# GEGLU feed-forward kernel: another order of the seven products in the gate/up loop, and one copy instead of two for the last output block

## Chip, cores, metric

The kernel runs on one core of one Trainium2 chip. The metric is device time in microseconds (us), as the median of several runs. The span of a profile, from the first to the last instruction, is some 1.8 us shorter than the time of the same run (277.88 against 276.1 us before).

Names of the engines in the profile: PE is TensorE, which does the matmuls; PEld its weight loads; DVE is VectorE; ACT is ScalarE; POOL is GpSimd; SP is SyncE. The granted clock is the share of the full TensorE clock that the chip allowed; it is 1.0 or just below in every run here. A PSUM bank is a piece of the memory into which matmuls add. fp32r is the kernel's four-byte type for matmuls (`float32r`); the profile prints it as f32.

A verdict needs 2%. The change is worth less than that, so most of this document works in nanoseconds inside the profile, where the parts of the kernel that the change does not touch agree to a few nanoseconds from kernel to kernel.

## The reference, cut to what matters

```python
B, S, D, F = 32, 32, 1024, 3584          # all bf16
def reference(x, w_gate, w_up, w_down):
    return (_gelu(x @ w_gate) * (x @ w_up)) @ w_down
```

With tokens flattened, `x` is 1024 x 1024, gate and up are 1024 x 3584, down is 3584 x 1024.

## The kernel before

The kernel replaces eight block products by seven (a Strassen-Winograd scheme), once for gate and up together and once for down. The first four feature tiles are computed plainly. The other 24 go through the gate/up loop, and that is where the change is. A feature tile has seven products of four matmuls each, 128x128 weights against 128x512 moving data. Five take sums in fp32r, two take the bf16 inputs as they are. Condensed to the products, with comments of mine:

```python
# in one feature tile ft (cut); names P1..P7 are used below
prod(psa, a11, b11, True)      # P1  bf16   -> copied by ACT (sn1), then P6 adds onto the bank
prod(psc, s1, t1, True)        # P5  fp32r  -> copied by ACT (sn5), then P3 adds onto the bank
last_product(open_ft)          # P4  fp32r  (a22, t4) of the tile before, onto its psa
prod(psa, s2, t2, False)       # P6  fp32r  -> copied by ACT (sn2)
prod(psc, s4, b22r, False)     # P3  fp32r  -> DVE: c12 = sn2 + psc; ACT: gelu
prod(psb, a12, b21, True)      # P2  bf16   -> DVE: c11 = sn1 + psb; ACT: gelu
prod(psa, s3, t3, False)       # P7  fp32r  -> DVE: c22 = sn5 + psa, times the gelu
```

`psa` is one of three PSUM banks, `psb` and `psc` each one of two. P1, P6, P7 and P4 of a tile all add onto one `psa`, each after the copy or the read of what stood there. `snap` is a copy by ACT, `added` a sum by DVE. POOL meanwhile makes the sums s1 to s4 of the next two tiles.

The last output block, after the last product of the down projection:

```python
for m in range(MT):                                  # four blocks of 128 rows
    o = opool.tile([P, NB], bf16, name="o_sb", tag="o_sb")
    r0 = NB + m * P
    for i, (cast, eng) in enumerate(((nc.scalar.copy, nc.sync), (nc.vector.tensor_copy, nc.scalar))):
        c = slice(i * NB // 2, (i + 1) * NB // 2)
        cast(o[:, c], banka[m][:, c])
        eng.dma_start(out=of[r0 : r0 + P, c], in_=o[:, c])
```

Of the kernel before, what the change touches and what calls it, by code (L numbers as in the profile page):

```python
# [13 lines left out]
def kernel(  # L14
# [20 lines left out]
    nc = tc.nc  # L35
    P = nc.NUM_PARTITIONS
# [7 lines left out]
    of = out.flatten_outer_dims()  # L44
    N, D = xf.shape
    F = w_gate.shape[1]
    NB = 512
    assert N == 2 * NB and D == 2 * NB and F % (4 * P) == 0
    DT, FT = D // P, F // P
    KD = DT // 2  # L50
    FC = 2
    F0 = 4
# [46 lines left out]
    def g_of(ft):  # L99
        k = ft % HF  # L100
        return by_batch(g_lo if ft < HF else g_hi)(k)

    def acc(tag):
        return ps1.tile([P, NB], fp32, name=f"ps{tag}", tag=tag, bufs={"A": 3, "B": 2, "C": 2, "G": 1}[tag])


    b11 = xpool.tile([P, KD, NB], bf16, name="b11")
    b21 = xpool.tile([P, KD, NB], bf16, name="b21")
    b12 = ring.tile([P, KD, NB], bf16, name="b12", tag="ring")
    b22 = ring.tile([P, KD, NB], bf16, name="b22", tag="ring")  # L110
    t1, t2, t3, t4, b22r = (xpool.tile([P, KD, NB], f32r, name=n) for n in ("t1", "t2", "t3", "t4", "b22r"))
# [21 lines left out]
    def load_w_chunk(ci):  # L133
        alloc_w(ci)
        for which in (0, 1):
            load_w(nc.sync, ci, which, 0, DT)

    def quads(ci, fl=None):
        cols = slice(None) if fl is None else slice(fl * P, (fl + 1) * P)
        wg, wu = w_tiles[ci]  # L140
        return wg[:, :KD, cols], wg[:, KD:, cols], wu[:, :KD, cols], wu[:, KD:, cols]

    def chunk_of(ft):
        ci, fl = divmod(ft - F0, FC)
        return ci + 1, fl
# [3 lines left out]
    def sums(ci, eng):  # L149

        a11, a12, a21, a22 = quads(ci)
        s1, s2, s4, s3 = (
            spool.tile([P, KD, FC * P], f32r, name=n, tag=n) for n in ("s1", "s2", "s4", "s3")
        )
        s_tiles[ci] = (s1, s2, s3, s4)
        yield eng.tensor_tensor(s1, a21, a22, ADD)  # L156
        yield eng.tensor_tensor(s2, s1, a11, SUB)  # L157
        yield eng.tensor_tensor(s4, a12, s2, SUB)  # L158
        yield eng.tensor_tensor(s3, a11, a21, SUB)  # L159
# [3 lines left out]
    def a22r_of(ft):  # L163
        t = spool.tile([P, KD, P], f32r, name="a22r", tag="a22r", bufs=3)
        nc.scalar.copy(t, quads(*chunk_of(ft))[3])  # L165
        a22rs[ft] = t
# [10 lines left out]
    with tc.manual_schedule():  # L177
        for eng, p0, p1 in ((nc.sync, 0, HALF), (nc.scalar, HALF, NB_P)):
            eng.dma_start(  # L179
                out=x_nat[:, p0:p1, :],  # L180
                in_=xf[p0 * P : p1 * P, : KQ * P].rearrange("(b p) d -> p b d", p=P),
# [84 lines left out]
        def prod(ps, lhs, rhs, start):  # L266
            for k in range(KD):
                nc.tensor.matmul(  # L268
                    ps,
                    lhsT=lhs[:, k, :],  # L270
                    rhs=rhs[:, k, :],
                    start=(start and k == 0),
                    stop=(k == KD - 1),
                    skip_group_check=True,
                )

        def snap(ps, tag, bufs):
            t = ework.tile([P, NB], fp32, name=tag, tag=tag, bufs=bufs)
            nc.scalar.copy(t, ps)  # L279
            return t  # L280

        def added(s, ps):
            t = ework.tile([P, NB], fp32, name="c", tag="c", bufs=3)
            tt(t, s, ps, ADD)  # L284
            return t

        def last_product(st):
            ft, psa, h0 = st
            prod(psa, a22rs.pop(ft), t4, False)
            tt(g_of(ft)[:, :NB], h0, psa, MUL)  # L290

        open_ft = None
        for ft in range(F0, FT):
            ci, fl = chunk_of(ft)
            fs = slice(fl * P, (fl + 1) * P)
            if fl == 0:
                nxt = sums(ci + 1, nc.gpsimd) if ci + 1 < NCH else iter(())
                if ci + 2 < NCH:
                    load_w_chunk(ci + 2)
            a11, a12, a21, a22 = quads(ci, fl)  # L300
            s1, s2, s3, s4 = (s[:, :, fs] for s in s_tiles[ci])
            psa, psc, psb = acc("A"), acc("C"), acc("B")
            prod(psa, a11, b11, True)
            sn1 = snap(psa, "sn1", 2)
            prod(psc, s1, t1, True)
            sn5 = snap(psc, "sn5", 2)
            if ft + FC < FT:
                a22r_of(ft + FC)
            if open_ft:
                last_product(open_ft)  # L310
            next(nxt, None)
            prod(psa, s2, t2, False)
            sn2 = snap(psa, "sn2", 1)
            prod(psc, s4, b22r, False)
            c12 = added(sn2, psc)
            h1 = acc("G")
            nc.scalar.activation(h1, c12, ACT.Gelu_apprx_tanh)  # L317
            prod(psb, a12, b21, True)
            c11 = added(sn1, psb)
            h0 = ework.tile([P, NB], bf16, name="h", tag="h")  # L320
            nc.scalar.activation(h0, c11, ACT.Gelu_apprx_tanh)
            next(nxt, None)
            prod(psa, s3, t3, False)
            c22 = added(sn5, psa)
            tt(g_of(ft)[:, NB:], c22, h1, MUL)
            open_ft = (ft, psa, h0)
# [84 lines left out]
        banka = [acc(t) for t in "AAAG"]  # L411
# [70 lines left out]
        for m in range(MT):  # L482
            o = opool.tile([P, NB], bf16, name="o_sb", tag="o_sb")
            r0 = NB + m * P
            for i, (cast, eng) in enumerate(((nc.scalar.copy, nc.sync), (nc.vector.tensor_copy, nc.scalar))):
                c = slice(i * NB // 2, (i + 1) * NB // 2)
                cast(o[:, c], banka[m][:, c])  # L487
                eng.dma_start(out=of[r0 : r0 + P, c], in_=o[:, c])
# [1 line left out]
_INS = ['x', 'w_gate', 'w_up', 'w_down']  # L490
_OUTS = [((32, 32, 1024), 'bfloat16')]
# [25 lines left out]
```

## Time and profile before

| | before |
|---|---|
| device time | 278.07 us, 3 runs, 277.82 to 278.48 |
| span of the profile | 276.1 us, granted clock 1.0 |
| start to start of two feature tiles | 6.327 us in the steady loop |
| last matmul's start to the span's end | 4.00 us |

The page of the kernel before: busy time of each engine (us, share of the span, instructions), and below it the first line of the chain of waits that ended last.

```profile
PE 271.4 (98%) x1207; PEld 182.5 (66%) x1207; DVE 173.3 (63%) x186; ACT 117.1 (42%) x181; POOL 94.8 (34%) x51
...
PE 96%; DMA 2%; ACTq 0%; DVE 0%; ACT 0%; issue 0%
```

TensorE (PE) bounds the kernel: the others have time to spare, and the chain hardly leaves PE. A busy PE is not a PE at its best pace, though. Ends of matmuls are estimated: so says the Trainium skill, "Perfetto Trace Analysis", section "Tensor Engine Instruction (MATMUL, LD_WEIGHTS)". This trace fits it. Matmuls that start 227 ns apart are each shown as 389 ns long. The section covers weight loads too, so the lengths of weight loads below are lengths in the profile and not measured times. So busy time and mean duration say nothing of the pace, and one has to look at starts.

The timeline of PE, before: start (us), length, line, operation, tiles, shape, count. One row is one product.

```profile
103.25 1.07 PE L268 MATMUL psA<-t,a22r 128*128 128x512 f32 x4
104.15 1.07 PE L268 MATMUL psA<-t,s 128*128 128x512 f32 x4
105.06 1.07 PE L268 MATMUL psC<-b22r,s 128*128 128x512 f32 x4
105.97 1.04 PE L268 MATMUL psB<-b,wg 128*128 128x512 bf16 x4
106.66 1.28 PE L268 MATMUL psA<-t,s 128*128 128x512 f32 x4
107.78 1.04 PE L268 MATMUL psA<-b,wg 128*128 128x512 bf16 x4
108.46 1.27 PE L268 MATMUL psC<-t,s 128*128 128x512 f32 x4
109.57 0.62 PE L268 MATMUL psA<-t,a22r 128*128 128x512 f32 x2
```

These are P4, P6, P3, P2, P7, P1, P5 and P4 again (the end of the window cuts the last row); bf16 comes in two groups of four, which I call islands. The first P7 matmul after an island appears to start only 0.69 us after the island's first, and then to last longer. That is an early-recorded start, not a fast product: island and following product together take 1.81 us (105.97 to 107.78).

Weight loads on the page of before, in bf16 and in fp32r: count, busy us, mean ns of one, idle before.

```profile
L268 PEld LDWEIGHTS <-wg 128*128 128x128 bf16 x192 | 15.0, 98 | 24.0 <-issue 12.5
...
L268 PEld LDWEIGHTS psA<-t,a22r 128*128 128x128 f32 x96 | 18.0, 188 | 3.9
```

The waits of weight loads in the loop, before: us in total, times, longest.

```profile
PEld L268 <- issue: 12.5, 47, 0.3
...
PEld psA L268 <- ACT sn L279: 0.2, 1, 0.2
PEld psC L268 <- ACT sn L279: 0.2, 1, 0.2
```

A bf16 load takes 98 ns, an fp32r load 188 ns. The Trainium skill, "TensorE: Matmul & The Clock Gate", section "Weight-path perf modes — Fast Weight Load (FWL) and DoubleRow", has the fast load on for 128 weights that are not FP32, with about a factor of two measured. The page does not say whether fp32r counts as FP32; the ratio in this trace, 188 to 98 or 1.9, fits if it does. The 47 "issue" waits mark the 47 places in the loop where fp32r gives way to bf16. Only two waits in the whole loop are for another engine, both at its start.

The timeline at the end, before: ACT copies its half, DVE waits for ACT, then the second store is issued.

```profile
272.53 0.37 ACT L487 CAST o_sb<-psG 128x256 bf16<-128x256 f32 x1 [1.21 <-PE psG L346]
272.93 0.33 SPq L488 DMA_DIRECT2D out_dram<-o_sb  x1
272.93 0.42 DVE L487 CAST o_sb<-psG 128x256 bf16<-128x256 f32 x1 [1.16 <-ACT o_sb L487]
273.39 0.34 ACTq L488 DMA_DIRECT2D out_dram<-o_sb  x1
```

### The profile page before, as it was taken

The page shows a single profiled execution, that of the slowest core. Times are in us where ns is not written, and L with a number is a line of the kernel's source. Part 1 is how long each engine was busy: PE and PEld are TensorE (multiplying, and loading weights), DVE is VectorE, ACT ScalarE, POOL GpSimd, SP SyncE. Part 2 cuts the span into 40 slices and gives each one's busy share as a digit, 9 for nine tenths or more (in the row PEclk, how much of TensorE's full clock was granted, in tenths as well). Part 3 has the DMA queues.
Part 4 walks back from the last instruction along what each step waited for, and adds up shares of the span by engine and source line. Part 5 has one row for each costly group of instructions (what it writes and reads, how often), then busy time and mean ns, then how long its engine had stood idle before and what let it go on. Part 6 is the DMA issues. An engine that isn't in the chain of part 4 may idle for free.

```text
span 276.1 us, 3300 instructions
## 1 busy us (share of the span) xinstructions
PE 271.4 (98%) x1207; PEld 182.5 (66%) x1207; DVE 173.3 (63%) x186; ACT 117.1 (42%) x181; POOL 94.8 (34%) x51
## 2 busy tenths in 40 slices
PE   8999999999999999999999999999999999999994
PEld 3444467666666777776666667754447888888883
DVE  0059975455555554554555555546999999999501
ACT  4034465555655555556556555430200022972001
POOL 1000069996765849494947650000000000000000
PEclk9999999999999999999999999999999999999999
DMA  7999023150505143250508500004992344686202
GB/s 156 318 249 263 3 76 104 51 154 0 154 1 151 34 118 96 58 143 10 154 0 251 168 2 1 0 0 135 348 318 76 111 155 167 234 271 206 77 6 70
DMA packets 52768, 33.77 MB, mean 122 GB/s; under 512 B 8720, under 2 KB 52752, under 8 KB 52752
## 3 DMA queue, kind: packets, MB, share of 16 engines
q1 hardware_dynamic: 49760, 31.20, 39.3%
q10 hardware_dynamic: 2992, 2.36, 2.8%
q8 instruction: 9, 0.15, 0.2%
q14 instruction: 7, 0.06, 0.1%
HBM read 29.62 MB, written 2.10 MB: 115 GB/s over the span
## 4 chain that ended last, share of the span: by engine, by line
PE 96%; DMA 2%; ACTq 0%; DVE 0%; ACT 0%; issue 0%
PE psA L268 32%; PE psC L268 16%; PE psA L346 14%; PE psB L268 8%; PE psB L346 7%; PE psC L346 7%; PE psG L346 5%; PE psA L221 4%; PE psB L221 3%; PE psC L221 2%; DMA wu<-in_w_up_dram 2%; PE psG L221 1%; ACTq L131 0%; ACTq L179 0%; DVE o_sb L487 0%; ACT o_sb L487 0%
## 5 line engine op out<-in xcount | busy, mean ns | idle before, releaser
L268 PE MATMUL psA<-t,s 128*128 128x512 f32 x192 | 56.4, 416 | 0.0
L268 PEld LDWEIGHTS psA<-t,s 128*128 128x128 f32 x192 | 36.1, 188 | 9.6 <-ACT sn L279 0.2
L279 ACT COPY sn<-psA 128x512 f32<-128x512 f32 x48 | 28.2, 588 | 21.5 <-PE psA L268 21.5
L156 POOL TENSOR_TENSOR s<-wu 128x1024 fp32r<-128x1024 bf16 x11 | 23.6, 2146 | 29.8 <-PE psC L268 29.8
L284 DVE TENSOR_TENSOR c<-sn,psC 128x512 f32<-128x512 f32 x24 | 16.5, 688 | 25.9 <-PE psC L268 25.9
L268 PEld LDWEIGHTS <-wg 128*128 128x128 bf16 x192 | 15.0, 98 | 24.0 <-issue 12.5
L268 PE MATMUL psC<-t,s 128*128 128x512 f32 x96 | 30.5, 439 | 0.0
L268 PE MATMUL psA<-t,a22r 128*128 128x512 f32 x96 | 25.9, 391 | 0.0
L268 PE MATMUL psC<-b22r,s 128*128 128x512 f32 x96 | 25.7, 389 | 0.0
L317 ACT ACTIVATE psG<-c 128x512 f32<-128x512 f32 x24 | 14.5, 602 | 25.6 <-DVE c L284 25.6
L268 PE MATMUL psB<-b,wg 128*128 128x512 bf16 x96 | 24.9, 382 | 0.0
L268 PE MATMUL psA<-b,wg 128*128 128x512 bf16 x96 | 24.9, 381 | 0.0
L158 POOL TENSOR_TENSOR s<-wg,s 128x1024 fp32r<-128x1024 bf16 x11 | 23.7, 2156 | 0.9
L157 POOL TENSOR_TENSOR s<-s,wg 128x1024 fp32r<-128x1024 f32 x11 | 23.6, 2146 | 0.9
L159 POOL TENSOR_TENSOR s<-wg,wu 128x1024 fp32r<-128x1024 bf16 x11 | 23.6, 2145 | 0.0
L290 DVE TENSOR_TENSOR hi<-h,psA 128x512 bf16<-128x512 bf16 x14 | 9.6, 688 | 19.5 <-PE psA L268 19.5
L268 PEld LDWEIGHTS psC<-t,s 128*128 128x128 f32 x96 | 18.1, 189 | 5.5
L268 PEld LDWEIGHTS psA<-t,a22r 128*128 128x128 f32 x96 | 18.0, 188 | 3.9
L268 PEld LDWEIGHTS psC<-b22r,s 128*128 128x128 f32 x96 | 17.9, 188 | 3.8 <-ACT sn L279 0.2
L284 DVE TENSOR_TENSOR c<-sn,psA 128x512 f32<-128x512 f32 x24 | 16.5, 688 | 5.8 <-PE psA L268 5.8
L284 DVE TENSOR_TENSOR c<-sn,psB 128x512 f32<-128x512 f32 x24 | 16.5, 687 | 2.8
L165 ACT CAST a22r<-wu 128x512 fp32r<-128x512 bf16 x24 | 14.9, 622 | 6.8 <-PE psA L268 6.8
(100 smaller groups left out, 419.8 us busy)
## 6 DMA issues: line engine op xcount, KB each, us to landing
wg<-in_w_gate_dram SPq DMA_DIRECT2D x12, 512.0 KB, 3.9
wu<-in_w_up_dram SPq DMA_DIRECT2D x12, 512.0 KB, 5.1
wdb<-in_w_down_dram SPq DMA_DIRECT2D x12, 512.0 KB, 4.7
wdb<-in_w_down_dram SPq DMA_DIRECT2D x12, 384.0 KB, 4.3
v<-in_w_down_dram SPq DMA_DIRECT2D x4, 512.0 KB, 6.1
v<-in_w_down_dram SPq DMA_DIRECT2D x4, 384.0 KB, 7.1
out_dram<-o_sb ACTq DMA_DIRECT2D x12, 128.0 KB, 1.7
wg<-in_w_gate_dram SPq DMA_DIRECT2D x3, 256.0 KB, 3.8
```

The costliest lines, as they stand in the source:

```text
L156: yield eng.tensor_tensor(s1, a21, a22, ADD)
L157: yield eng.tensor_tensor(s2, s1, a11, SUB)
L158: yield eng.tensor_tensor(s4, a12, s2, SUB)
L159: yield eng.tensor_tensor(s3, a11, a21, SUB)
L165: nc.scalar.copy(t, quads(*chunk_of(ft))[3])
L221: nc.tensor.matmul(ps, lhsT=w_tiles[0][which][:, dt, fl * P : (fl + 1) * P], rhs=x_rows(dt, nb), start=(dt == 0), stop=(dt == DT - 1),)
L268: nc.tensor.matmul(ps, lhsT=lhs[:, k, :], rhs=rhs[:, k, :], start=(start and k == 0), stop=(k == KD - 1), skip_group_check=True,)
L279: nc.scalar.copy(t, ps)
L284: tt(t, s, ps, ADD)
L290: tt(g_of(ft)[:, :NB], h0, psa, MUL)
L317: nc.scalar.activation(h1, c12, ACT.Gelu_apprx_tanh)
L346: nc.tensor.matmul(banks[m], lhsT=lhs(k)[:, m * P : (m + 1) * P], rhs=rhs(k), start=(start and k == 0), stop=(k == HF - 1), skip_group_che ...
```

## The change

Its intent: P2 of a tile and P1 of the next stand side by side, so that TensorE changes between bf16 and fp32r twice a tile instead of four times. P6 goes ahead of P4 as well. The last block is copied whole, by DVE and ACT in turn, and stored by one queue.

```diff
+        def first_product(ft):
+            psa = acc("A")
+            prod(psa, quads(*chunk_of(ft))[0], b11, True)
+            return psa, snap(psa, "sn1", 2)
+
         open_ft = None
+        ahead = first_product(F0)
         for ft in range(F0, FT):
   ... (cut)
-            psa, psc, psb = acc("A"), acc("C"), acc("B")
-            prod(psa, a11, b11, True)
-            sn1 = snap(psa, "sn1", 2)
+            (psa, sn1), psc, psb = ahead, acc("C"), acc("B")
             prod(psc, s1, t1, True)
             sn5 = snap(psc, "sn5", 2)
+            next(nxt, None)
+            prod(psa, s2, t2, False)
+            sn2 = snap(psa, "sn2", 1)
             if ft + FC < FT:
                 a22r_of(ft + FC)
             if open_ft:
                 last_product(open_ft)
-            next(nxt, None)
-            prod(psa, s2, t2, False)
-            sn2 = snap(psa, "sn2", 1)
             prod(psc, s4, b22r, False)
   ... (cut)
             next(nxt, None)
+
+            if ft + 1 < FT:
+                ahead = first_product(ft + 1)
             prod(psa, s3, t3, False)
   ... (cut)
-            for i, (cast, eng) in enumerate(((nc.scalar.copy, nc.sync), (nc.vector.tensor_copy, nc.scalar))):
-                c = slice(i * NB // 2, (i + 1) * NB // 2)
-                cast(o[:, c], banka[m][:, c])
-                eng.dma_start(out=of[r0 : r0 + P, c], in_=o[:, c])
+            (nc.vector.tensor_copy if m % 2 == 0 else nc.scalar.copy)(o, banka[m])
+            nc.scalar.dma_start(out=of[r0 : r0 + P, :NB], in_=o)
```

More of the change, by code (lines that the diff above doesn't have):

```diff
@@ L299 @@
                     load_w_chunk(ci + 2)
-            a11, a12, a21, a22 = quads(ci, fl)
             s1, s2, s3, s4 = (s[:, :, fs] for s in s_tiles[ci])
-            psa, psc, psb = acc("A"), acc("C"), acc("B")
-            prod(psa, a11, b11, True)
-            sn1 = snap(psa, "sn1", 2)
+            (psa, sn1), psc, psb = ahead, acc("C"), acc("B")
             prod(psc, s1, t1, True)
             sn5 = snap(psc, "sn5", 2)
+            next(nxt, None)
+            prod(psa, s2, t2, False)
+            sn2 = snap(psa, "sn2", 1)
             if ft + FC < FT:
@@ L317 @@
             nc.scalar.activation(h1, c12, ACT.Gelu_apprx_tanh)
-            prod(psb, a12, b21, True)
+            prod(psb, quads(ci, fl)[1], b21, True)
             c11 = added(sn1, psb)
```

## The prediction

> **What bounds the kernel now.** TensorE. The page gives PE 98% of the span at granted clock 1.0; the chain of waits is 96% PE; DVE, ACT and POOL are busy 63%, 42% and 34%. In the gate/up loop (32.7 to 183.7 us, 24 feature tiles of 28 matmuls) PE never waits for another engine but for two 0.2 us waits of weight loads at its start. Moving products can help only through what matmuls themselves cost, and hurt only by a new wait.
>
> **What the matmuls cost.** Ends of matmuls are modelled (the Trainium skill, "Perfetto Trace Analysis", section "Tensor Engine Instruction"), so I use distances between starts in the timeline. A feature tile takes 6.327 us in every steady iteration. Within fp32r products a matmul follows the last by 227 ns (weight load 188 ns); within bf16 products by 216 ns (weight load 98 ns). The shorter bf16 load agrees with "TensorE: Matmul & The Clock Gate", section "Weight-path perf modes": fast weight load is on for 128 weights that are not FP32. Pure pace would be 20 x 227 + 8 x 216 = 6.26 us. The other 65 ns are four changes of type: into bf16 the first two distances are 230 and 226; out of it 454 for two, then 233, 236 (or 231), 228. A bf16 island costs some 23 to 38 ns over its pace. There are 47 islands (the weight loads' "issue" idle: 47 times, 12.5 us; not PE time).
>
> **What the change does.** No matmul or copy of the loop is added or removed. P2 of a tile and P1 of the next form one island of eight, so 23 islands go. Built from the distances of before, an iteration becomes 6.29 to 6.30 us: 27 to 38 ns less, times 23 = 0.6 to 0.9 us, all on the critical path.
>
> **New waits?** I find none. Between P1 and P6 (which must wait for the copy of P1's bank) still lie two products, 1.8 us. ACT does that copy after the second gelu: ending 2.2 us after P2's end, with P6 starting 2.7 us after it: 0.5 us of slack, the tightest of all. P5 to P3, and P7 to P4, keep two products between; P6 to P7 gets four. Three A banks suffice. POOL's sums (four of 2.15 us in 12.65 us) end in time.
>
> **The tail.** Before, the two half copies of the last block run in series, since both write one tile: ACT 372 ns, then DVE 424 ns, then issue, 1.62 us to landing. After: one ACT copy of 512 columns (588 ns for that shape elsewhere), then a 128 KB store, 1.70 to 1.74 us to landing. 0.21 saved less 0.1: about 0.1 us gained.
>
> **Prediction.** 278.07 - 0.75 - 0.1 = 277.2 us, 8 in 10 within 276.6 to 277.8. Faster by over 2%: 1%; within 2%: 97%; slower by over 2%: 2%.
>
> **What would show the steps right or wrong.** Iteration distance 6.29 to 6.30 us; "issue" idle of weight loads 24 times, not 47; 216 ns across the seam P2 to P1; no wait of PE or its loads for ACT or DVE in the loop; last ACT copy about 0.59 us, the span's end about 0.1 us closer to the last matmul.
>
> **What would make it wrong.** A PE wait for the copy of P1 (ACT order) repeated 23 times: each 0.1 us would cost 2.3 us. Then: P7 after an island dearer than P5, which puts the gain at the lower end. Or a tail in which the ACT queue holds up the last copy behind an issue (0.34 us each).

## The result, and the profile after

| | before | after |
|---|---|---|
| device time, median | 278.04 us, 6 runs, 277.16 to 278.48 | 276.83 us, 6 runs, 276.33 to 277.01 |
| span of the profile | 276.1 us | 275.2 us |
| start to start of two feature tiles | 6.327 us | 6.300 us |
| last matmul's start to the span's end | 4.00 us | 3.61 us |

The ratio is 0.9958, 95% interval 0.9941 to 0.9975: the mean time of the fast runs after over that of the fast runs before in the same rounds, so not quite the ratio of the two medians. The time is inside the predicted range, and the sign is clear of noise.

The page after, the same lines:

```profile
PE 270.1 (98%) x1190; PEld 184.3 (67%) x1207; DVE 173.1 (63%) x184; ACT 114.4 (42%) x179; POOL 94.9 (34%) x51
...
PE 98%; issue 0%; ACT 0%
```

PE lacks 17 of its 1207 matmul records here; the weight loads are complete, so I take iteration times from the loads of P4. The timeline of PE, after:

```profile
103.92 1.07 PE L268 MATMUL psA<-t,a22r 128*128 128x512 f32 x4
104.82 1.07 PE L268 MATMUL psC<-b22r,s 128*128 128x512 f32 x4
105.73 1.04 PE L268 MATMUL psB<-b,wg 128*128 128x512 bf16 x4
106.61 1.03 PE L268 MATMUL psA<-b,wg 128*128 128x512 bf16 x4
107.28 1.27 PE L268 MATMUL psA<-t,s 128*128 128x512 f32 x4
108.39 1.08 PE L268 MATMUL psC<-t,s 128*128 128x512 f32 x4
109.31 1.07 PE L268 MATMUL psA<-t,s 128*128 128x512 f32 x4
110.22 0.62 PE L268 MATMUL psA<-t,a22r 128*128 128x512 f32 x2
```

P4, P3, then P2 and P1 as one island, P7, P5, P6. The next P4 comes 6.30 us after the first. The waits of weight loads in the loop, after:

```profile
PEld L268 <- issue: 6.3, 24, 0.3
...
PEld psA L268 <- ACT sn L279: 0.2, 1, 0.2
PEld psC L268 <- ACT sn L279: 0.2, 1, 0.2
```

ACT's timeline around the copy of P1's bank, after:

```profile
101.23 0.63 ACT L324 ACTIVATE h<-c 128x512 bf16<-128x512 f32 x1 [0.21 <-DVE c L284]
101.77 0.57 ACT L279 COPY sn<-psA 128x512 f32<-128x512 f32 x1
```

24 changes into bf16 instead of 47, and no new wait for another engine. The tightest dependence, P1's copy by ACT, ends at 102.34 us; P6 of that tile starts at 103.01 us, so 0.67 us are left, as in every steady tile (0.67 or 0.68 us). The end, after:

```profile
271.97 0.58 ACT L491 CAST o_sb<-psG 128x512 bf16<-128x512 f32 x1 [2.59 <-PE psG L352]
272.59 0.34 ACTq L492 DMA_DIRECT2D out_dram<-o_sb  x1
```

**Where the time went.** The two profiles divide exactly into three parts (the down projection from its last gate/up product to the last matmul takes 85.158 us in both):

| part of the span (us) | before | after | difference |
|---|---|---|---|
| up to the loop's first weight load | 32.463 | 32.535 | +0.07 |
| from there to the first load of the last P4 | 154.484 | 153.856 | -0.63 |
| last matmul's start to the end | 3.999 | 3.609 | -0.39 |

The first row is noise: the program up to that point is the same, yet over the 14 kernels profiled the loop's first load came anywhere between 32.11 and 33.13 us. That is as much as the whole gain. One profile's span, or one time, therefore decides nothing here; iteration and tail do.

The tail's 0.39 us has three parts. From the start of ACT's last copy to the end of the last copy: 0.828 us before, 0.585 after (-0.243). From the issue of the last store to its landing: 1.619 and 1.718 (+0.099). From the landing to the span's end: 1.096 and 0.851 (-0.245). The third I had not foreseen. In the trace, SyncE closes the kernel by waiting for the DMA semaphores in a row. The records of its sequencer (start in us, semaphores waited for):

```
before: 275.025 (104)     275.083 (105, 103)  275.145 (106, 102)  275.209 (107, 100)  275.271 (108, 109)
after:  269.690 (105,102) 271.143 (106, 100)  272.837 (107, 109)  274.323 (108, 110)
```

The last store reports on semaphore 104 before, which is waited for first: four waits of about 62 ns each still follow. After the change it reports on 108, which is waited for last.

### The profile page after: what moved, and what is told of

Same layout as the page of the kernel before. It is cut to its first block, busy times and chain, and to the rows that moved or that the text cites. A ratio compares the mean times of both kernels' runs of the same rounds, so it can differ in the third digit from the quotient of the medians.

```text
span 275.2 us, 3268 instructions
## 1 busy us (share of the span) xinstructions
PE 270.1 (98%) x1190; PEld 184.3 (67%) x1207; DVE 173.1 (63%) x184; ACT 114.4 (42%) x179; POOL 94.9 (34%) x51
## 4 chain that ended last, share of the span: by engine, by line
PE 98%; issue 0%; ACT 0%
PE psA L268 31%; PE psC L268 16%; PE psA L352 14%; PE psB L268 7%; PE psB L352 7%; PE psC L352 7%; PE psG L352 5%; PE psA L221 4%; PE psC L221 3%; PE psB L221 3%; PE psG L205 1%; PE psG L221 1%; PE tp L213 0%; ACT o_sb L491 0%; PE psG L217 0%
## 5 line engine op out<-in xcount | busy, mean ns | idle before, releaser
L268 PEld LDWEIGHTS <-wg 128*128 128x128 bf16 x192 | 16.9, 98 | 23.3 <-issue 6.3
L268 PE MATMUL psC<-t,s 128*128 128x512 f32 x96 | 26.1, 394 | 0.0
L268 PE MATMUL psB<-b,wg 128*128 128x512 bf16 x84 | 22.2, 381 | 0.8
L279 ACT COPY sn<-psC 128x512 f32<-128x512 f32 x24 | 14.1, 589 | 20.3 <-PE psC L268 20.3
```

Of the source, the lines that this page charges most:

```text
L268: nc.tensor.matmul(ps, lhsT=lhs[:, k, :], rhs=rhs[:, k, :], start=(start and k == 0), stop=(k == KD - 1), skip_group_check=True,)
L279: nc.scalar.copy(t, ps)
```

## The experiments

Theory at this point: two separate gains, 0.63 us from fewer changes of type in the loop and 0.39 us from the tail. The rivals are named with each run. Runs with one time only (their state is unknown; the granted clock in their profiles is 0.999 or 1.0) are used for their profile alone. Nothing here rests on a slow run.

### The two parts alone

`loop_only` has the new loop and the old last block; `tail_only` the old loop and the new last block.

```diff
 loop_only, against after
-            (nc.vector.tensor_copy if m % 2 == 0 else nc.scalar.copy)(o, banka[m])
-            nc.scalar.dma_start(out=of[r0 : r0 + P, :NB], in_=o)
+            (the four lines of before)
```

> The new loop with the old last block. Theory (two separate gains): iteration of the gate/up loop 6.300 us as in the changed kernel (23 x 27 ns = 0.62 us gained), while the time from the last copy's start on ACT to the span's end stays 3.57 us as before; device time about 0.6 us (0.22%) under before. Rival (the loop explains the whole gain): about 1.2 us under before. Rival (the tail explains it all): no gain.

> The old loop with the new last block. Theory: iteration 6.327 us; last ACT copy's start to the span's end 3.18 us instead of 3.57 us, so about 0.39 us (0.14%) under before; the sum of the two single gains (0.6 + 0.4) makes up the gain of the whole change. Rival (my prediction's sum): 0.1 us.

| | iteration | loop part | start of ACT's last copy to the end | median | ratio to before, 95% interval |
|---|---|---|---|---|---|
| before | 6.327 | 154.484 | 3.574 | 277.67 (11 runs) | |
| loop_only | 6.300 | 153.860 | 3.570 | 277.22 (6 runs) | 0.9982, 0.9969 to 0.9995 |
| tail_only | 6.327 | 154.442 | 3.172 | 277.73 (5 runs) | 0.9998, 0.9984 to 1.0011 |

(The profile parts of before are those of its one profile.) In the profiles each part does what it does in the whole change, to within 0.05 us, and neither touches the other. The times agree with `loop_only`'s 0.62 us. For `tail_only` they show no gain; the 0.39 us of its profile (a ratio of 0.9986) is still inside the interval, at its edge. Its own profile shows why a time tells little: the loop began at 33.13 us, 0.67 us later than in before. So the tail's gain is shown in the profile and not in the times.

### Is it the number of islands, or the longer distances between dependent products?

`apart` keeps the new order but takes P1 of the next tile away from P2 and puts it between P4 and P3. `three` splits P1 into two halves, after P5 and after P4.

```diff
 apart, against after
             if open_ft:
                 last_product(open_ft)
+            if ft + 1 < FT:
+                ahead = first_product(ft + 1)
   ... (cut; the same two lines are removed in front of P7)
 three, against after
             sn5 = snap(psc, "sn5", 2)
             next(nxt, None)
+            if ft + 1 < FT:
+                ahead = acc("A")
+                prod_part(ahead, ft + 1, 0, 2)       # two matmuls of P1
   ... (cut; after P4:)
+            if ft + 1 < FT:
+                prod_part(ahead, ft + 1, 2, KD)      # the other two
+                ahead = ahead, snap(ahead, "sn1", 2)
   ... (cut; the call of first_product in front of P7 is removed)
```

> The new order with P1 of the next tile taken away from P2 and put between P4 and P3: again two bf16 islands in a tile, but P6 ahead of P4 and every dependent pair at least as far apart as in the changed kernel. Theory (the number of changes of type decides): iteration back to 6.327 us, at most 0.01 us off. Rival (the longer distances between dependent products, P6 to P7 above all, gave the gain): 6.300 us.

> P1 of the next tile in two halves of two matmuls, one after P5 and one after P4: three bf16 islands in a tile. Theory: each island more costs 25 to 30 ns, so 6.35 to 6.36 us an iteration, about 1.3 us over the changed kernel in the loop. Rival (cost goes with the bf16 matmuls, not with the islands, or comes from waits): 6.30 to 6.33 us.

`apart`: 6.327 us, as before to the nanosecond, though every pair of dependent products is as far apart as after the change or farther. So the order and the distances give nothing; bringing the islands together gives the 27 ns. `three`: 6.394 us, 67 ns over two islands, not the 25 to 30 I expected. The direction is right, but an island has no fixed price.

### What a wait would have cost

`late_p1` puts P1 of the next tile behind P7, so that P5 alone stands between P1 and P6.

```diff
             next(nxt, None)
-
-            if ft + 1 < FT:
-                ahead = first_product(ft + 1)
             prod(psa, s3, t3, False)
+            if ft + 1 < FT:
+                ahead = first_product(ft + 1)
```

> P1 of the next tile behind P7 instead of beside P2: two islands, and only one product (P5) between P1 and P6, which must wait until ACT has copied P1's bank. Theory: 6.327 us for the islands plus a wait of some 0.03 us (in the first iteration of before, where only one product stood between, the two products together took 0.03 us more), 6.33 to 6.38 us an iteration, with a wait of PE's loads for ACT in most iterations. Rival (one product is enough cover): 6.327 us and no waits.

It took 6.40 and 6.43 us in turn: 0.07 to 0.10 us over two islands. The waits of weight loads in this kernel (stretch of the loop from 60 to 180 us):

```profile
PEld L268 <- issue: 10.1, 38, 0.3
PEld psA L268 <- issue: 2.2, 9, 0.2
PEld psA L268 <- ACT sn L279: 1.7, 9, 0.2
```

In this stretch the load of P6 waits 18 times: nine waits are put down to ACT, and for the other nine the view names nothing, but there too the load starts just after the copy's end (copy to 122.83 us, load at 122.94 us). One product is not enough cover for ACT's copy, two are. The time is above the range that I expected (6.33 to 6.38 us): a wait that I had put at 0.03 us took two to three times as much. This was the risk that I named in the prediction; the change avoids it, because P7 and P5 stand between.

### No islands at all

`all_f32r` gives P1 and P2 the fp32r operands of P5 and P6 (a wrong result). `all_bf16` makes every fp32r tile of the kernel bf16, in one line; its sums are then rounded to bf16.

```diff
 all_f32r, against after
-            prod(psa, quads(*chunk_of(ft))[0], b11, True)
+            ci, fl = chunk_of(ft)
+            prod(psa, s_tiles[ci][0][:, :, fl * P : (fl + 1) * P], t1, True)
   ... (cut)
-            prod(psb, quads(ci, fl)[1], b21, True)
+            prod(psb, s2, t2, True)
 all_bf16, against after
-    f32r = mybir.dt.float32r
+    f32r = mybir.dt.bfloat16
```

> Wrong result on purpose: P1 and P2 take the fp32r sums as operands (P1 the operands of P5, P2 those of P6), so no bf16 matmul is left in the loop. Theory: 28 x 226.7 ns = 6.347 us an iteration, every distance 227 ns, no 'issue' idle of weight loads in the loop: 47 ns over the changed kernel. Rival (the changes of type cost nothing, the extra time is something else that stays, such as waits): 6.347 + 0.039 = 6.386 us.

> All fp32r tiles made bf16 (sums rounded to bf16; less exact, perhaps not passing). Theory: every matmul at the 216 ns pace, 28 x 216 = 6.05 us an iteration, no island left: 0.25 us x 24 = 6 us less in the loop, and some 3 us less in the down projection (about 280 of its fp32r matmuls at 227 ns), unless DVE or ACT now bound it. Rival (227 ns is set by the moving data's width or by bank traffic): iteration stays near 6.3 us.

`all_f32r`: 6.347 us an iteration, 28 x 226.67 ns, every distance 226 or 227 ns and no "issue" wait in the loop. So the extra time of the other kernels is tied to the changes of type and not to some wait that stays. `all_bf16`: 6.043 us, 28 x 215.8 ns; the down projection's part of 85.158 us shrank to 82.015; and 267.89 us in all (4 runs, ratio 0.9647, interval 0.9626 to 0.9667). The fp32r weight loads that took 188 ns are now like this (groups of instructions, same columns as above):

```profile
L268 PEld LDWEIGHTS <-s 128*128 128x128 bf16 x384 | 37.6, 98 | 45.3
```

It passed the comparison with the reference. It does less exact arithmetic than the other kernels, so it is a version to be weighed by how much error one may spend, not one of equal worth. Whether the 227 ns come from the weights' type or from the moving data's it does not tell: both changed. The same holds for the price of a change of type, since every run changes the two together.

With the two pure paces one can work out what the islands cost: 20 x 226.67 + 8 x 215.83 = 6260 ns would be a tile without any. Before: 67 ns more. After: 40 ns.

### What an island costs

`p2_alone` has one island of four (P1 takes fp32r operands; a wrong result). `far` has the two islands of four at a greater distance, P1 of the next tile between P6 and P4.

```diff
 p2_alone, against after
-            prod(psa, quads(*chunk_of(ft))[0], b11, True)
+            ci, fl = chunk_of(ft)
+            prod(psa, s_tiles[ci][0][:, :, fl * P : (fl + 1) * P], t1, True)
 far, against after
             sn2 = snap(psa, "sn2", 1)
+            if ft + 1 < FT:
+                ahead = first_product(ft + 1)
   ... (cut; the same two lines are removed in front of P7)
```

> Wrong result on purpose: P1 takes the fp32r operands of P5, so one island of four bf16 matmuls (P2) is left in a tile, followed by P1, P7, P5 and the rest, 24 fp32r matmuls. Theory (an island with enough fp32r matmuls after it has a fixed price, the 38 ns of the changed kernel's island of eight): 24 x 226.7 + 4 x 216 + 38 = 6.343 us. Rival (the price goes with the number of bf16 matmuls in it): half of 38, 6.324 us.

> P1 of the next tile between P6 and P4: two islands of four, with 8 fp32r matmuls (P4, P3) after the first and 12 (P7, P5, P6) after the second; in the kernel before it is 4 and 16. Theory (after an island it takes eight matmuls to get back to 227 ns, so that the two islands of before share part of the price: 65 ns instead of two times 38): apart they cost about 76 ns, 6.338 us. Rival (two islands cost 65 ns wherever they stand): 6.327 us.

Both came out dearer than theory and rival said. All loops together (price: iteration less the pure paces of its matmuls):

| kernel | islands in a tile | fp32r matmuls after each | iteration, ns | price, ns |
|---|---|---|---|---|
| all_f32r | none | | 6347 | 0 |
| p2_alone | 4 | 24 | 6367 | 63 |
| before | 4 and 4 | 4 and 16 | 6327 | 67 |
| apart | 4 and 4 | 4 and 16 | 6327 | 67 |
| far | 4 and 4 | 8 and 12 | 6380 | 120 |
| three | 2, 2 and 4 | 8, 4 and 8 | 6394 | 134 |
| after | 8 | 20 | 6300 | 40 |

An island of four on its own costs some 60 ns. Two of them cost 120 ns when eight and twelve fp32r matmuls follow, but only 67 ns when the second comes four matmuls after the first: then the pair costs hardly more than one alone. So the kernel before was already better than it looked. And an island of eight is cheaper (40 ns) than one of four.

The distances between starts of successive matmuls after an island (ns, means over steady iterations; the first is the one that begins 28 or 29 ns after the island's last record) show a pattern. I set them below each other so that like stands under like:

```
p2_alone               425 233 236 224 231 236 228 233 231 227 227 ...
far, after P2          418 229 234 236 224 231 235 229 232 231 227 ...
far, after P1          425 234 236 224 231 235 229 238 | bf16
before, after P2       425 233 236 228 | bf16
apart, after P1        425 233 236 228 | bf16
after                  417         224 231 236 228 233 231 226 227 ...
before, after P1       418                         232 231 227 227 ...
apart, after P2        418                         232 231 227 227 ...
```

The way back to 227 ns is much the same series each time, but it is joined at its start, after two steps, or near its end. It is not the product that decides where: in before it is P7 that follows the dear exit and P5 the cheap one; in `apart` P3 follows the dear one and P7 the cheap one. What sets the point of entry stays open. The number of fp32r matmuls before the island does not decide it either: after four of them the way back is short in before and in `apart` (418, 232, 231), but long in `three` after P2 (418, 229, 233, 236, 224, 231, 236, 232).

### The closing waits

`shift4` is the changed kernel with four stores, some 65 us before the end, sent as two halves each. That is four DMAs more, and the eight DMA semaphores are used in rotation.

```diff
-            nc.scalar.dma_start(out=of[r0 : r0 + P, col * NB : (col + 1) * NB], in_=o)
+            for i in range(2 if tok == col == 0 else 1):
+                n = NB // 2 if tok == col == 0 else NB
+                nc.scalar.dma_start(
+                    out=of[r0 : r0 + P, col * NB + i * n : col * NB + (i + 1) * n], in_=o[:, i * n : (i + 1) * n]
+                )
```

> The changed kernel with four earlier stores (those of the first down product, some 65 us before the end) sent as two halves each: four DMAs more, none near the end. Theory (the eight DMA semaphores are used in rotation and the end waits for them one after the other, so it matters how many waits stand after the one that the last store fulfils): the last landing falls on the first of five closing waits again as in before, last ACT copy's start to span's end 3.18 + 0.25 = 3.43 us. Rival (the closing got shorter because there are fewer DMAs at the end, or a single issuing queue): stays 3.18 us.

The start of ACT's last copy to the span's end took 3.468 us, 0.284 more than after the change. The last store now lands on semaphore 104, and the trace has four waits behind it again (274.651, then 274.720, 274.782, 274.846 and 274.907 us). From the landing to the end: 1.107 us, against 0.851 after and 1.096 before. So 0.25 us of the tail's gain is a matter of the number of DMAs modulo eight, and has nothing to do with who copies what. The remaining 0.03 us is a slower landing (1.745 us).

### Could the halves run side by side?

My prediction said that the two half copies run in series "since both write one tile". `halves88` gives them two tiles in the last of the four blocks, and joins two weight loads so that the number of DMAs stays 88. `bf16_halves88` has bf16 sums besides.

```diff
   ... (cut: the joined weight loads; the first three blocks stay as after the change)
+            o2 = opool.tile([P, NB], bf16, name="o_sb", tag="o_sb")
+            for t, cast, eng, i in ((o, nc.scalar.copy, nc.scalar, 0), (o2, nc.vector.tensor_copy, nc.sync, 1)):
+                c = slice(i * NB // 2, (i + 1) * NB // 2)
+                cast(t[:, c], banka[m][:, c])
+                eng.dma_start(out=of[r0 : r0 + P, c], in_=t[:, c])
```

> The changed kernel, but with the last block copied in halves by ACT and DVE into two tiles, so that the halves run side by side, and stored by two queues; two loads of a weight are joined in one so that the number of DMAs stays 88. Theory (the old halves ran in series only because they wrote one tile; 64 KB land 0.1 us sooner than 128 KB): copies end 0.43 us after the last product instead of 0.59, the span's end 2.9 us after the start of ACT's last copy instead of 3.18, iteration 6.300 us: about 0.27 us under the changed kernel, 1.3 us (ratio 0.9954) under the kernel before. Rival (something else makes the halves run in series, such as the shared bank): end at 3.4 us, no better than the old tail.

> The same tail with all fp32r tiles made bf16. Theory: iteration 6.044 us as in all_bf16, tail 2.9 us, so 0.25 us under all_bf16's 267.9 us: about 267.6 us, ratio to the kernel before about 0.964. Rival: the tail's gain does not show in the time at all (the launch's own end hides it): 267.9 us.

The end of `halves88` in the timeline:

```profile
272.19 0.37 ACT L503 CAST o_sb<-psG 128x256 bf16<-128x256 f32 x1 [2.59 <-PE psG L352]
272.60 0.34 ACTq L504 DMA_DIRECT2D out_dram<-o_sb  x1
272.60 0.42 DVE L503 CAST o_sb<-psG 128x256 bf16<-128x256 f32 x1 [1.30 <-ACT o_sb L503]
273.05 0.36 SPq L504 DMA_DIRECT2D out_dram<-o_sb  x1
```

DVE still waits for ACT. My reason was wrong: with two tiles the halves are as serial as before. In the trace DVE's copy waits for a semaphore that ACT's copy raises; what is still common to both is the PSUM bank that they read, but that it is the cause is argued, not shown. The start of ACT's last copy to the end took 3.272 us: better than the old tail's 3.574, almost wholly by the closing waits (landing to end 0.835 us instead of 1.096), and worse than the 3.184 of the change. The time was 277.23 us (6 runs; ratio to before 0.9968, interval 0.9956 to 0.9980). Between these two kernels the number of DMAs is the same, so 3.272 less 3.184, some 0.09 us, is an estimate of what the whole copy is worth without the closing waits: about the 0.1 us of the prediction. One whole copy is the better choice, for as long as halves can't overlap.

`bf16_halves88` took 267.76 us (5 runs; ratio 0.9633, interval 0.9620 to 0.9645). Its interval overlaps that of `all_bf16`, so nothing can be said between the two; the rival (267.9 us) did as well as the theory. Its tail is no shorter either: 3.295 us from the start of ACT's last copy to the end.

## Why the prediction was right or wrong

- **"What bounds the kernel now. TensorE": right.** The loop's 0.63 us appear one to one in the span: the 24 tiles shrink and nothing gives the time back.
- **"Within fp32r products a matmul follows the last by 227 ns, within bf16 products by 216": right,** and sharper with the pure loops: 226.67 and 215.83 ns. The bf16 figure is that of the Trainium skill ("TensorE: Matmul & The Clock Gate", section "Wait — 56ns, not 53.3ns?": 215.7 ns for 512 columns at full clock).
- **"A bf16 island costs some 23 to 38 ns over its pace": wrong as a rule.** The runs showed 40 ns for an island of eight, about 60 for a lone one of four, and 67 for two that stand four matmuls apart. I had split the 65 ns of a pair as if each island had its own share.
- **"27 to 38 ns less, times 23 = 0.6 to 0.9 us": right, at its lower end** (27 ns, 0.63 us). It held because I built the new iteration from distances of before and did not subtract a price per island. The gain is 67 less 40, the difference between two whole patterns. That the figure fits so well is in part luck: the way back in the new loop (417, 224, 231, 236, 228, 233, 231) is neither of the two that the loop before showed (425, 233, 236, 228 and 418, 232, 231); only its sum is near that of the dearer one.
- **"P7 after an island dearer than P5": wrong in its cause.** The dear exit exists, but `apart` shows that it goes with the place and not with the product.
- **"New waits? I find none": right.** The slack of P1's copy was 0.67 us where I had estimated 0.5. `late_p1` shows what one product less of cover costs: 0.07 to 0.10 us a tile, some 2 us in all.
- **"The tail ... about 0.1 us gained": mis-sized; it measured 0.39 us.** Copies (0.21 said, 0.243 measured) and landing (0.1 said, 0.099 measured) were right. The term that I left out is the closing chain of semaphore waits, 0.245 us, as `shift4` shows. The reason that I gave for the serial halves, one tile, fell with `halves88`.
- **The sum:** 0.85 us said; 0.63 + 0.39 = 1.02 us in the profiles; 1.2 us between the medians. The difference of the last two is within the spread of runs, whose start alone varies by up to 1 us. The range held because the two errors, loop 0.12 us too large and tail 0.29 us too small, are small against its width of 1.2 us. They also have opposite signs; that they partly cancel is luck.

## What to carry to other kernels

When TensorE is full and nothing waits, read starts of matmuls and not their lengths: where types change, a few distances are longer, and grouping products by type removes some of that; but count whole patterns, because the price depends on what stands around the change. Check first that each copy between dependent products keeps its cover: one product was too little here, two were enough. At the very end of a kernel, look at what follows the last landing too; and before polishing changes worth 0.4%, test whether the types themselves can change, which gave 3.5% here (`all_bf16`, the new order included), some eight times as much, at the price of less exact sums.

## What the Trainium skill lacked or had wrong

- "TensorE: Matmul & The Clock Gate" gives no pace for fp32r, and nothing on what a change of type between neighbouring matmuls costs. Here fp32r matmuls of 128x512 follow each other by 226.67 ns against 215.83 ns in bf16, and going into bf16 and out again costs 40 to 63 ns for one island in a loop of 28 matmuls.
- The same page, section "LDWEIGHTS (loading the stationary operand)", gives columns divided by 1.2, so 107 ns for 128 columns. In the profile the fp32r loads here are 188 ns long, the bf16 ones 98 ns (lengths with an estimated end).
- The same page, section "Back-to-back issue gap", puts a sustained stream of loads and matmuls at about 131 ns for 512 columns. The densest stream here, all bf16, never went under 215 ns from start to start in the steady loop, as the 215.7 ns of the page's other section has it.
- I found no page with the closing chain of a kernel: SyncE waits for the DMA semaphores one after the other, about 62 ns each, so that the number of DMAs modulo eight moved the end by 0.25 us.
